# Every engine takes the computed order: one manually scheduled region around a whole attention and MLP kernel

## The chip, the core and the metric

The kernel runs on one core of a Trainium2 chip. Five engines work side by side, each through its own list of instructions: TensorE (PE, matrix products, with its weight loads PEld), VectorE (DVE), ScalarE (ACT), GpSimd (POOL) and SyncE (SP, here only the issue of DMAs). They wait for each other through semaphores. Each engine takes the instructions of its list in the order in which they stand there, so an instruction that waits holds up all that stand behind it on its engine.

The metric is the device time of one execution in microseconds (us), as the median of several runs; lower is better.

## What is computed

Linear attention with random features over 8 batches, 8 heads, 576 positions and head size 64, and an MLP with a Silu over the result, all in float32:

```python
def phi(x):
    proj = np.einsum('bhsd,md->bhsm', x, omega)          # 128 features
    h = proj - np.sum(x * x, axis=-1, keepdims=True) / 2.0
    h = h - np.max(h, axis=-1, keepdims=True)
    return np.exp(h) / np.sqrt(m)
q_p, k_p = (phi(q_s), phi(k_s))                          # q, k scaled by D ** -0.25
kv = np.einsum('bhsm,bhsd->bhmd', k_p, v)
z = np.sum(k_p, axis=2)
num = np.einsum('bhsm,bhmd->bhsd', q_p, kv)
den = np.einsum('bhsm,bhm->bhs', q_p, z)[..., None] + 1e-06
attn = num / den
...
x = attn.transpose(0, 2, 1, 3).reshape(B * S, H * D)     # 4608 x 512
h = x @ w_in                                             # 512 x 2048
g = h * (1.0 / (1.0 + np.exp(-h)))
out = g @ w_out                                          # 2048 x 512
```

## The kernel before

The attention is cut into 32 windows, one for a batch and a pair of heads. A window goes through these steps, each a small function: load `raw` (k and q, transposed, line 238), `nat` (k and q by rows, 242) and `v` (246) on SP; squares on ACT (250) and their row sums on DVE (254); the projection on PE (262, and 269 for the middle block); row maxima (276, 278) and the shift `nb` (282, 283) on DVE; the exponentials on ACT (298, from window 8 on 312); the sums of k's features over the positions on POOL (318 to 323) and their product with ones on PE, `z` (327), copied by ACT into `zb` (335, 336); `kv` on PE (343), copied into `kt` (348), turned (351) and copied into `kw` (356); the products of q's features with z on DVE (362), their sums `den` and reciprocals `rd` (369, 370); the normalization on POOL (375); three transposes on PE (381), copied into `en` (385); and the numerator (399), which ACT and DVE split into a high and a low part `xh`, `xl` (413, 418).

Four windows give the input of one block of 512 rows of the MLP, so there are eight blocks, and a ninth from the rests of 64 rows (`rest`, 423, stored and loaded again). A block takes 16 steps, one for each 128 columns of `w_in`: stage 1 (495, twelve matmuls into `ps_h`), Silu twice on ACT (500 for the high part `gh`, 501 in place), the low part `gl` on DVE (505), and two steps later stage 2 (513, twelve matmuls into `ps_acc`). In the first block the weights are prepared too: load `wraw` on SP (435), exponent on ACT (442), three DVE instructions (456, 458, 462), split on POOL into `wh`, `wl` (or `wp`, which is stored, 483, and fetched for every step, 487).

ACT needs a table load to go from an exponential to a Silu or back.

What sets the order: about 3,600 units (`add(name, engine, duration, due, ...)`) go to a planner, the class `Plan`. It walks through time with a free time for each engine, looks at what each unit needs and which buffers are free, and gives back one list of all units. The kernel then emits the units in that list's order. Before the change this is not yet the order on the engines: the library's scheduler takes the emitted instructions, with the emission as a priority, and decides by its own model of when things are ready what stands where on each engine.

Of the kernel before, what the change touches and what calls it, by code (L numbers as in the profile page):

```python
# [197 lines left out]
def attention_mlp(ctx: ExitStack, tc: tile.TileContext, qT, kT, qn, kn, v, om_in, w_in, w_out, out):  # L198
# [6 lines left out]
    pools = {  # L205
        p: ctx.enter_context(tc.tile_pool(name=f"ps_{p}", bufs=RINGS[p], space=PSUM)) for p in ("acc", "h", "att")
    }
# [13 lines left out]
    def bank(pool):  # L221
        return pools[pool].tile([P, 512], F32, tag=pool, name=f"ps_{pool}")
# [310 lines left out]
    plan = Plan()  # L533
# [155 lines left out]
    for i, (t, f) in enumerate(steps):  # L689
# [16 lines left out]
        for j in range(4):  # L706
# [11 lines left out]
            if f == NF - 1:  # L718
                add(("store", t, j), "ACT", 0.62, k2 + 0.2, lambda t=t, j=j: store(t, j), after=[("s2", t, f, j)],
                    free=[("po", t, j)])  # L720
    for u in plan.run():
        u["fn"](*[bank(p) for p in u["pools"]])


_OUT = ((B * S, DMODEL), "float32")
# [48 lines left out]
```

## Time and profile before

| | us |
|---|---|
| median of 3 runs | 1099.16 (1097.70 to 1101.51) |
| profiled execution | 1101.4 |
| its span, from the first to the last instruction | 1099.3 |
| PE busy | 1053.1 (96%) |
| DVE busy | 566.4 (52%) |
| ACT busy | 583.1 (53%) |
| POOL busy | 255.5 (23%) |

An engine's busy time is the union of its instructions' times. In a row of instructions in order of time the first number is the start in us from the span's start, the second the length of the row; then engine, line, operation, the tile written and the tiles read, and in brackets the idle time of the engine just before it and whose event ended it. A row of waits gives the sum of the waits, their count and the longest one. ACT's table loads number 48 at line 312, 56 at line 500, 11 at line 298, 4 at line 501 and 1 at line 232.

### The profile page before, as it was taken

Reading aid. Unit: us, or ns where it says so; the run is one execution under the profiler, and the core shown is the slowest. Engines: PE = TensorE matmul, PEld = TensorE weight load, DVE = VectorE, ACT = ScalarE, POOL = GpSimd, SP = SyncE. Lnnn points to the kernel's source line nnn. Section 1 sums busy time; section 2 is a strip of 40 time slices with the busy share of each in tenths; the row PEclk is TensorE's granted clock in tenths of the full one; section 3 lists DMA queues with packets and bytes.
Section 4 is the critical chain, followed back from the end, with each engine's and each line's share of the span. In section 5 each row is a group of like instructions: output and inputs, shape, how many; then the busy total and the mean of one; then the engine's idle time right before and its main releaser. Section 6 shows DMA issues by size and latency. Waiting matters only on the chain.

```text
span 1099.3 us, 16192 instructions
## 1 busy us (share of the span) xinstructions
PE 1053.1 (96%) x5900; PEld 834.5 (76%) x5900; DVE 566.4 (52%) x1109; ACT 583.1 (53%) x1085; POOL 255.5 (23%) x327
## 2 busy tenths in 40 slices
PE   5677998899999999999999999999999999999998
PEld 4455776687877778777778777787877788888886
DVE  6788897745555455545555455555554431111111
ACT  5557878565556555555556555655565442222211
POOL 3666665411111111111111111111111110000000
PEclk7688999999999999999999999999999999999999
DMA  7576787553335443444345433533343226223323
GB/s 282 198 221 234 265 290 252 182 167 125 124 126 178 139 133 119 136 165 138 122 139 178 140 127 130 173 131 126 123 154 104 80 80 213 96 96 122 109 96 96
DMA packets 66526, 167.84 MB, mean 153 GB/s; under 512 B 15632, under 2 KB 15760, under 8 KB 66448
## 3 DMA queue, kind: packets, MB, share of 16 engines
q1 hardware_dynamic: 65984, 166.23, 45.6%
q8 instruction: 47, 0.77, 0.3%
q10 hardware_dynamic: 464, 0.59, 0.1%
q14 instruction: 31, 0.25, 0.1%
HBM read 146.87 MB, written 19.92 MB: 152 GB/s over the span
## 4 chain that ended last, share of the span: by engine, by line
PE 86%; DVE 5%; DMA 3%; ACT 3%; POOL 1%; issue 1%; SPq 0%; ACTq 0%; DVEq 0%; POOLq 0%
PE ps_acc L513 35%; PE ps_h L495 34%; PE ps_att L262 5%; PE ps_att L343 3%; PE ps_att L381 3%; PE ps_att L399 2%; DMA wraw<-w_out 1%; DMA nat<-qn 1%; PE ps_att L327 1%; PE ps_att L269 1%; DVE w L458 1%; ACT hq L298 1%; DVE w L462 1%; POOL hq L375 1%; DVE den L369 1%
## 5 line engine op out<-in xcount | busy, mean ns | idle before, releaser
L513 PE MATMUL ps_acc<-wo,gh 128*128 128x512 f32 x1152 | 369.9, 402 | 0.0
L500 ACT ACTIVATE gh<-ps_h 128x512 fp32r<-128x512 f32 x144 | 86.2, 599 | 295.9 <-PE ps_h L495 295.3
L505 DVE TENSOR_TENSOR gl<-ps_h,gh 128x512 fp32r<-128x512 f32 x144 | 99.1, 688 | 275.8 <-ACT ps_h L501 275.8
L513 PEld LDWEIGHTS ps_acc<-wo,gh 128*128 128x128 f32 x1152 | 207.1, 189 | 43.7
L495 PE MATMUL ps_h<-xh,wh 128*128 128x512 f32 x576 | 235.0, 409 | 0.3 <-ACT xh L413 0.3
L495 PE MATMUL ps_h<-xh,wl 128*128 128x512 f32 x576 | 226.7, 394 | 0.0
L495 PE MATMUL ps_h<-xl,wh 128*128 128x512 f32 x576 | 225.9, 392 | 0.0
L513 PE MATMUL ps_acc<-wo,gl 128*128 128x512 f32 x576 | 225.8, 392 | 0.0
L375 POOL TENSOR_TENSOR hq<-hq,rd 128x384 f32<-128x384 f32 x96 | 81.7, 879 | 421.4 <-DVE rd L370 396.5
L495 PEld LDWEIGHTS ps_h<-xh,wh 128*128 128x128 f32 x576 | 108.1, 188 | 24.7 <-issue 0.8
L513 PEld LDWEIGHTS ps_acc<-wo,gl 128*128 128x128 f32 x576 | 108.1, 188 | 24.2 <-issue 0.8
L495 PEld LDWEIGHTS ps_h<-xh,wl 128*128 128x128 f32 x576 | 108.1, 188 | 24.1
L495 PEld LDWEIGHTS ps_h<-xl,wh 128*128 128x128 f32 x576 | 108.5, 188 | 22.3 <-DVE xl L418 0.4
L312 ACT ACT_TABLE_LOAD x48 | 61.6, 1283 | 69.2 <-DVE hq L303 53.3
L318 POOL TENSOR_TENSOR t<-hk 128x256 f32<-128x256 f32 x64 | 48.8, 780 | 183.2 <-ACT hk L312 170.1
L278 DVE TENSOR_REDUCE mxq<-ps_att 128x4 f32<-128x512 f32 x57 | 37.2, 687 | 99.7 <-PE ps_att L262 99.6
L501 ACT ACTIVATE ps_h<-ps_h 128x512 f32<-128x512 f32 x144 | 85.3, 593 | 0.0
L500 ACT ACT_TABLE_LOAD x56 | 71.8, 1283 | 22.0 <-PE ps_h L495 21.3
L362 DVE TENSOR_TENSOR prod<-hq,zb 128x512 f32<-128x512 f32 (+1 forms) x96 | 52.3, 595 | 49.6 <-ACT zb L336 47.7
L250 ACT ACTIVATE nat<-nat 128x576 f32<-128x576 f32 x64 | 44.6, 703 | 20.3 <-DMA nat<-kn 12.3
L381 PE MATMUL ps_att<-ident,hq 128*128 128x128 f32 x261 | 41.1, 284 | 7.9 <-POOL wp L476 2.4
L278 DVE TENSOR_REDUCE mxk<-ps_att 128x4 f32<-128x512 f32 x55 | 35.6, 686 | 18.7 <-PE ps_att L262 18.7
(121 smaller groups left out, 1232.0 us busy)
## 6 DMA issues: line engine op xcount, KB each, us to landing
wo<-wo_d SPq DMA_DIRECT2D x144, 512.0 KB, 3.3
rawk<-kT SPq DMA_DIRECT2D x32, 352.0 KB, 3.0
rawq<-qT SPq DMA_DIRECT2D x32, 352.0 KB, 3.8
v<-v SPq DMA_DIRECT2D x32, 320.0 KB, 2.9
nat<-kn SPq DMA_DIRECT2D x32, 288.0 KB, 3.3
nat<-qn SPq DMA_DIRECT2D x32, 288.0 KB, 3.2
wraw<-w_in SPq DMA_DIRECT2D x16, 512.0 KB, 4.6
wraw<-w_out SPq DMA_DIRECT2D x16, 512.0 KB, 4.3
```

Source lines behind the costliest of these rows:

```text
L262: nc.tensor.matmul(ps[:, i * M : (i + 1) * M], raw[r, o : o + P], oms[r], start=True, stop=True)
L278: nc.vector.tensor_reduce(m[:, 5 * j : 5 * j + 4], ps.rearrange("p (c m) -> p c m", m=M), AX.X, ALU.max)
L312: nc.scalar.activation(h, h, AF.Exp)
L318: nc.gpsimd.tensor_tensor(t[:, j], e[:, 5 * j : 5 * j + 2], e[:, 5 * j + 2 : 5 * j + 4], ALU.add)
L362: nc.vector.tensor_tensor(prod[:, c, :M], e[:, c], zb[:, j].unsqueeze(1).broadcast_to([P, hi - lo, M]), ALU.mult)
L375: nc.gpsimd.tensor_tensor(e[:, c], e[:, c], rd[:, c].unsqueeze(2).broadcast_to([P, 3, M]), ALU.mult)
L381: nc.tensor.transpose(ps[:, i * P : (i + 1) * P], T["h", n, "q"][:, 3 * g + i], ident)
L495: nc.tensor.matmul(ph, w[:, k, :], x, start=k == 0 and n == 0, stop=k == NK - 1 and n == 2)
L500: nc.scalar.activation(gh, ph, AF.Silu)
L501: nc.scalar.activation(ph, ph, AF.Silu)
L505: nc.vector.tensor_tensor(gl, T["ph", t, f], T["gh", t, f].bitcast(F32), ALU.subtract)
L513: nc.tensor.matmul(T["po", t][j], g[:, js], w, start=f == 0 and n == 0, stop=f == NF - 1 and n == 2)
```

## The change

The loop that emits the units goes into one region of the library in which every engine issues its instructions in the order of emission. Nothing else differs; the planner, its costs and its list are the same.

```diff
-    for u in plan.run():
-        u["fn"](*[bank(p) for p in u["pools"]])
+    with tc.manual_schedule():
+        for u in plan.run():
+            u["fn"](*[bank(p) for p in u["pools"]])
```

So the planner's list now stands on every engine, where the library's scheduler had moved units or parts of units. From the middle of the second MLP block on the two orders are almost the same on PE, ACT and POOL; most differences lie in the first block and ahead of it. Three places:

PE, the list's rows near its start, where the transposes of window 0 (line 381) end and window 1 goes on; `es` are POOL's sums, `kt` the copy of kv. Before:

```order
L381 MATMUL ps_h<-ident,hq 128x128 x3
L381 MATMUL ps_att<-ident,hq 128x128 x6
L327 MATMUL ps_h<-es,ones 128x256
L343 MATMUL ps_att<-hk,v 64x128 x10
L399 MATMUL ps_acc<-en,kw 64x512 x2
L399 MATMUL ps_att<-en,kw 64x64 x2
L262 MATMUL ps_acc<-oms,rawk 128x128 x8
L351 MATMUL ps_acc<-ident,kt 128x128
```

and now:

```order
L381 MATMUL ps_h<-ident,hq 128x128 x3
L381 MATMUL ps_att<-ident,hq 128x128 x6
L343 MATMUL ps_att<-hk,v 64x128 x10
L399 MATMUL ps_acc<-en,kw 64x512 x2
L399 MATMUL ps_att<-en,kw 64x64 x2
L262 MATMUL ps_acc<-oms,rawk 128x128 x8
L351 MATMUL ps_acc<-ident,kt 128x128
L327 MATMUL ps_h<-es,ones 128x256
```

The z product of window 1 (line 327) stood ahead of kv, of the numerator of window 0 and of the projection of window 2's k; now it stands behind them and behind the turn of kv.

ACT, windows 3 and 4; the squares (line 250) are those of q of window 6, `kt` and `kw` are window 4's. Before:

```order
L298 ACTIVATE hk<-ps_acc,nbk 128x128
L250 ACTIVATE nat<-nat 128x576
L348 COPY kt<-ps_acc 128x128
L356 COPY kw<-ps_acc 128x128
L298 ACTIVATE hq<-ps_att,nbq 128x128 x8
L385 COPY en<-ps_att 128x384
```

and now:

```order
L298 ACTIVATE hk<-ps_acc,nbk 128x128
L348 COPY kt<-ps_acc 128x128
L298 ACTIVATE hq<-ps_att,nbq 128x128 x8
L385 COPY en<-ps_att 128x384
L356 COPY kw<-ps_acc 128x128
L385 COPY en<-ps_att 128x384 x2
```

The square is gone from here (it stands behind the numerator's copies, lines 413, now), and `kw` goes behind the eight exponentials.

ACT, window 6 and steps 6 and 7 of the first MLP block; `hk` is the exponential of the middle block. Before:

```order
L500 ACT_TABLE_LOAD
L500 ACTIVATE gh<-ps_h 128x512
L298 ACT_TABLE_LOAD
L298 ACTIVATE hk<-ps_att,nbk 128x128
L501 ACT_TABLE_LOAD
L501 ACTIVATE ps_h<-ps_h 128x512
L385 COPY en<-ps_att 128x384
```

and now:

```order
L298 ACTIVATE hk<-ps_att,nbk 128x128
L500 ACT_TABLE_LOAD
L500 ACTIVATE gh<-ps_h 128x512
L501 ACTIVATE ps_h<-ps_h 128x512
L385 COPY en<-ps_att 128x384
```

The exponential stood between the two Silu activations of a step; now the pair stays together. This happened in four steps; no such place is left, and ACT has eight table loads fewer.

In words, on the other engines: on DVE `den` of window 2 (line 369) stood behind the square sum of window 4's q (line 254), and now stands ahead of it; the two DVE rows of `nb`, and `den` and `rd`, stood apart with other rows between them, and now stand together. On POOL the five rows of a window's sums had weight rows between them in windows 1, 4, 5 and 6, and now have none. On PE six matmuls of line 495 of step 1 stood ahead of the transposes of window 2, and now stand behind two of the three of window 4. On SP some loads of `raw`, `v` and `nat` and the stores of `rest` change places with the loads of weights.

## The prediction, made before the changed kernel ran

> **What bounds the kernel now.** I read the page's busy shares first, then the busy time by stage, then who waits for whom on TensorE, and last the instructions in order of time around each long wait.
>
> ```profile
> PE 1053.1 (96%) x5900; PEld 834.5 (76%) x5900; DVE 566.4 (52%) x1109; ACT 583.1 (53%) x1085; POOL 255.5 (23%) x327
> ```
>
> TensorE (PE) is the bound over the whole. Whether it is so everywhere, the stages tell (from and to, the length, then PE's busy time and matmuls, weight loads, DVE, ACT, POOL, the granted clock of TensorE and the share of the DMA engines):
>
> ```profile
> 28.20:101.10 72.90, 51.36 (x316) 34.54 (x317) 59.75 (x108) 44.50 (x134) 48.42 (x55) 0.76 0.66 213
> ...
> 118.30:216.00 97.70, 89.43 (x495) 67.28 (x494) 82.84 (x137) 72.34 (x137) 59.54 (x60) 1.00 0.72 247
> 245.60:1086.00 840.40, 840.19 (x4693) 675.38 (x4693) 374.88 (x767) 412.15 (x704) 122.73 (x179) 1.00 0.40 130
> ```
>
> From 245.6 to 1086 us PE lacks 0.2 us of 840.4. Nothing that leaves its work alone can make that shorter, and its rows stand in nearly the same order in both kernels. What can be had lies ahead of it: 72.90 - 51.36 = 21.5 us of PE idle time in the first row and 97.70 - 89.43 = 8.3 in the second. The time up to 28.2 us has the same order on every engine but for pairs that change nothing for PE. So the question is how many of these 29.8 us the new order takes away, and whether it adds others. The two longest single waits of PE after 28 us (in all, times, longest) are ended by POOL's sums and by one of ACT's copies:
>
> ```profile
> PE ps_h L327 <- POOL es L323: 5.5, 1, 5.5
> PE ps_acc L351 <- ACT kt L348: 3.0, 1, 3.0
> ```
>
> **The change, place by place.** No instruction is added but markers, and PE, DVE and POOL do the same work. Every term is therefore a wait of one engine's row for another, and each is a question of what stands ahead of what.
>
> *Term 1, window 1.* PE has the z product of window 1 (line 327) ahead of the kv and numerator products, and it waits for POOL's sums:
>
> ```profile
> 33.65 1.22 PE L327 MATMUL ps_h<-es,ones 128*128 128x256 f32 x2 [5.50 <-POOL es L323]
> ...
> 45.43 0.90 PE L381 MATMUL ps_acc<-ident,hq 128*128 128x128 f32 x3 [2.69 <-POOL hq L375]
> ```
>
> In the new order kv, the numerator and the next projection come first and fill those 5.50 us. The sums end when they did (POOL's rows up to them only change places), so z still starts at 33.65; what it feeds comes earlier, because ScalarE's (ACT) copies of z stood behind `kt`, which waited for kv:
>
> ```profile
> 37.25 0.27 ACT L348 COPY kt<-ps_att 128x128 f32<-128x128 f32 x1 [6.71 <-PE ps_att L343]
> ...
> 39.92 0.27 ACT L336 COPY zb<-ps_h 128x128 f32<-128x128 f32 x1
> ...
> 42.33 1.35 DVE L369 TENSOR_REDUCE den<-prod 128x9 f32<-128x1161 f32 x1
> ...
> 44.20 0.21 DVE L370 RECIPROCAL rd<-den 128x9 f32<-128x9 f32 x1
> ```
>
> z ends at 33.65 + 1.22 = 34.87; four copies take about 1.1 (0.27 each), so 35.9. The three products take 1.59 when they stand together (the row of window 2 below), to 37.5, then `den` 1.35, so `rd` can start near 38.8 where it stood at 44.20: 5.4 us earlier, and with it POOL's three normalizations and the transposes at 45.43. PE's own wait gives the same size from the other side (5.50). **5.4 us.**
>
> *Term 2, window 2.* VectorE (DVE) has the square sum of a later window ahead of `den`, and that one waits, by way of ACT's square, for a load that the chain of what ended last shows (its start, its length):
>
> ```profile
> 53.83 4.20 DMA nat<-qn
> ...
> 55.83 1.59 DVE L362 TENSOR_TENSOR prod<-hq,zb 128x512 f32<-128x512 f32 x3
> 58.83 0.76 DVE L254 TENSOR_REDUCE sqq<-nat 128x9 f32<-128x576 f32 x1 [1.41 <-ACT nat L250]
> 59.50 1.35 DVE L369 TENSOR_REDUCE den<-prod 128x9 f32<-128x1161 f32 x1
> ...
> 61.37 0.20 DVE L370 RECIPROCAL rd<-den 128x9 f32<-128x9 f32 x1
> ```
>
> In the new order `den` and `rd` follow the products at once: `rd` at 57.42 + 1.27 (1.35 less the overlap of 0.08 that these rows show) = 58.7 instead of 61.37, **2.7 us**. The load's lateness then falls on the square sum, which is wanted only by the exponentials two windows on. Against it stands that PE filled a part of this wait with six matmuls of line 495, which the new order puts later:
>
> ```profile
> 57.68:59.23 1.55, 1.55 (x7) 0.94 (x5) 0.40 (x1) 1.01 (x2) 0.00 (x0) 1.00 0.83 164
> ```
>
> They fill the 1.55 us of this stretch (the seventh runs in from before) and are still to be done: **minus 1.5**.
>
> *Term 3, window 4.* ACT has a square (line 250), whose load lands late, ahead of the copy `kt` (line 348), for which PE's line 351 waits:
>
> ```profile
> 84.22 0.68 ACT L250 ACTIVATE nat<-nat 128x576 f32<-128x576 f32 x1 [4.07 <-DVE mxk L278]
> 84.81 0.25 ACT L348 COPY kt<-ps_acc 128x128 f32<-128x128 f32 x1
> ...
> 80.76 1.31 PE L343 MATMUL ps_acc<-hk,v 128*64 128x128 f32 x20
> ```
>
> The kv products end at 82.07, so `kt` can run there and not at 84.81: **2.7 us**, and the square goes behind, where its load has long landed. What is late next is the exponential of the same window's q, about 2 us behind; the three transposes after it keep a wait.
>
> Up to 101 us that is 5.4 + 2.7 - 1.5 + 2.7 = 9.3 of the 21.5 us of idle time. From 101.1 to 118.3 PE was full and stays so.
>
> *Term 4, windows 5 to 7 (118 to 216 us).* ACT's pair of Silu activations (lines 500, 501) is torn apart four times by one exponential, and a pair torn apart costs two table loads more:
>
> ```profile
> L501 ACT ACT_TABLE_LOAD  x4: 1283/1283/1283, 139.5 to 190.4; - x4
> ```
>
> In the new order no pair is torn apart: 8 x 1.283 = 10.3 us of ACT's time go. How much of it PE sees, no row tells; the bounds are 0 (ACT is busy 72 of 97.7 us, and the idle time may come from elsewhere) and the 8.3 us that PE idles there. Neither end is nearer to a row, so I take the middle, **4.1**.
>
> Costs that I put at nothing: dependent pairs on DVE now stand back to back; DVE is busy 375 of 840 us where PE is full, which hides them. SP's loads move by one to four places; what that can cost is rival 4.
>
> Sum: 9.3 + 4.1 = 13.4 us. The profiled execution took 1101.4 us (span 1099.3 and 2.1 around it), so it would be 1088.0; the median of the runs is 1099.16, 2.2 below it, which gives 1085.8. **I forecast 1086.**
>
> **A rule weighed.** DVE's first product of window 6 took far longer than its second, which has the same form, while POOL worked beside it:
>
> ```profile
> 150.18 1.75 DVE L362 TENSOR_TENSOR prod<-hq,zb 128x512 f32<-128x512 f32 x1 [0.64 <-ACT zb L336]
> ...
> 152.05 0.68 DVE L362 TENSOR_TENSOR prod<-hq,zb 128x512 f32<-128x512 f32 x1
> ```
>
> The Trainium skill, page "SBUF — State Buffer", section "Who interferes with whom", says that the port pair which DVE and GpSimd share is an exclusive lock: a DVE instruction with two SBUF inputs and a GpSimd instruction do not share it, the later one waits to the end. The trace agrees in kind (1.75 against 0.68). By that rule the change has a price of its own, since the same DVE and POOL work is packed into fewer microseconds; it would bring about the first rival.
>
> **The rivals.**
>
> *1. The weights set the pace.* Between 118 and 216 us DVE is busy 82.84 of 97.7 us, mostly with the words of the weights, and POOL makes of them what PE reads. If DVE and POOL finish no weight earlier than now, step 13 of the MLP cannot start before its weight:
>
> ```profile
> 181.58 1.30 POOL L480 TENSOR_TENSOR wl<-w,wh 128x512 fp32r<-128x512 f32 x1
> ...
> 191.40 0.50 PE L495 MATMUL ps_h<-xh,wh 128*128 128x512 f32 x1
> ```
>
> 191.40 - 182.88 = 8.5 us is then all that can be gained: 1099.2 - 8.5 = 1090.7, and 1095 where a product row's excess of 1.07 us (1.75 - 0.68, above) is paid once more in each of four windows. Against it: DVE also gets free time back, since rows that waited for loads no longer block it.
>
> *2. More than I count.* If the new order removes all 8.3 us after 118 and 5 of the 12.2 us that I leave before 101, the gain is 9.3 + 8.3 + 5 = 22.6: 1076.6.
>
> *3. The wait only moves.* PE meets the window's normalizations later instead of the sums, with the chain over DVE and POOL as long as before: 1099. Against it: `rd` is shown above to be late because of its neighbours, not of its own inputs.
>
> *4. Slower: SP's queue.* In the new order SP's loads of raw q and the stores of `rest` stand ahead of weight loads that now pass them (the stores of `rest` of window 5 ahead of three, the load of `rawq` of window 8 ahead of one). These wait in the same stretch (101 to 216 us) for:
>
> ```profile
> SPq L238 <- PE ps_att L269: 13.9, 5, 5.2
> ...
> SPq L423 <- DVE xl L418: 4.0, 3, 2.1
> ```
>
> If all 17.9 us came on top of the weights' times, step 13 would start at 182.9 + 17.9 = 200.8 instead of 191.4: 9.4 us later, 1108.6. It decides from 8.5 + 3.3 = 11.8 us of added delay on. Against it: SP waits for mid products that themselves come earlier.
>
> That the change does nothing can be left out: the order differs on all five engines.
>
> **How the numbers follow.** Chances: the forecast with its own range 1081 to 1091, 0.60; rival 1, 0.18; rival 2, 0.10; rival 3, 0.05; rival 4, 0.07. A measurement of this kernel can tell about 0.3% from no change, 3.3 us, so faster is below 1095.9 and slower above 1102.5. The forecast and rivals 1 and 2 are faster: 0.88; same 0.05; slower 0.07. The range takes in rivals 1 and 2 and leaves 3 and 4 out: 1076.5 to 1096.5.
>
> **What would show it.** Term 1: no idle time before line 327, and the transposes of window 1 near 40 instead of 45.4 us. Term 2: `rd` right behind `den` in window 2, some 8 us earlier than 61.4 with term 1. Term 3: `kt` of window 4 right behind kv. Term 4: no table load at line 501, and PE idle time of about 4 us where it was 8.3. From there to the end PE must be full and as long as before, 840 us from the numerator of window 8 on; if that stretch is longer, the new order has a wait in every window and I am wrong in the part that I held safe. Rival 4 would show as idle time before line 495 or 513 with a DMA or POOL's weights as its end.

## The result, and the profile after

The changed kernel takes **1090.57 us** (median of 4 runs, 1089.20 to 1091.57) where the kernel before, on the same chip, took 1099.2: a ratio of 0.992, with a 95% interval of 0.9907 to 0.9933. That is 8.6 us where 13.4 had been worked out. The profiled execution took 1089.6 us, its span is 1087.5. Busy times of the whole, from the page:

```profile
PE 1040.2 (96%) x5900; PEld 825.2 (76%) x5900; DVE 572.1 (53%) x1109; ACT 574.3 (53%) x1077; POOL 254.6 (23%) x327
```

ACT has eight instructions fewer, the table loads. PE has the same 5900 matmuls and is busy 12.9 us less (1053.1 before). The stages of the changed kernel, in the columns of the prediction (from and to, length, busy time of PE, PEld, DVE, ACT, POOL, granted clock, DMA share, GB/s):

```profile
28.20:94.50 66.30, 44.78 (x301) 31.04 (x298) 64.95 (x106) 46.41 (x137) 43.83 (x50) 0.74 0.70 227
...
111.50:203.90 92.40, 84.15 (x495) 64.07 (x494) 83.67 (x138) 62.49 (x130) 56.87 (x59) 1.00 0.75 252
233.10:1073.50 840.40, 839.68 (x4694) 673.37 (x4694) 367.76 (x767) 414.31 (x704) 122.75 (x179) 1.00 0.41 130
```

Three things are to be seen. The last row is as long as before: the part held safe was safe. The first row is 6.6 us shorter, and DVE is now busy 64.95 of its 66.30 us (98%; 59.75 of 72.90 before). And in the second row PE's idle time is what it was: 92.40 - 84.15 = 8.25 us, before 97.70 - 89.43 = 8.27. The row is 5.3 us shorter because the *same 495 matmuls take 5.3 us less busy time*. The prediction had asked only for idle time. The first row has the idle time that it had, too: 66.30 - 44.78 = 21.52 us, before 72.90 - 51.36 = 21.54. But its two stretches hold 301 and 316 matmuls; a comparison over the same matmuls stands in the part on why the prediction was right.

Which matmuls? The same stretches again, with the busy time of the projections (line 262) alone, before and then after:

```profile
118.30:216.00 97.70, 11.29 (x96) 1.00 0.72 247
```

```profile
111.50:203.90 92.40, 7.24 (x96) 1.00 0.75 252
```

4.05 of the 5.3 us are there. A projection is eight calls, emitted in pairs: for each of four groups of columns one for the first head and one for the second, which read rows 0 to 63 and rows 64 to 127 (`r = slice(j * D, (j + 1) * D)`). The trace has two matmuls for a call, so 16 for a projection; this stretch holds three projections of k and three of q. PE's rows of a projection of q before,

```profile
139.70 1.16 PE L262 MATMUL ps_att<-oms,rawq 64*128 64x128 f32 x8
140.78 0.50 PE L495 MATMUL ps_h<-xh,wl 128*128 128x512 f32 x1
...
142.05 0.40 PE L495 MATMUL ps_h<-xl,wh 128*128 128x512 f32 x1
142.38 1.16 PE L262 MATMUL ps_att<-oms,rawq 64*128 64x128 f32 x8
```

and now:

```profile
192.63 0.39 PE L495 MATMUL ps_h<-xh,wl 128*128 128x512 f32 x1
192.95 1.16 PE L262 MATMUL ps_att<-oms,rawq 64*128 64x128 f32 x16
194.04 0.50 PE L495 MATMUL ps_h<-xh,wh 128*128 128x512 f32 x1
```

In the three projections of q the library's scheduler had pulled the two heads apart, with matmuls of line 495 between them: eight of one head take 1.16 us, twice. In the order of emission the heads alternate, and sixteen take the same 1.16 us (1.43 in the slowest projection of this stretch): a matmul in one half of the array's rows runs beside one in the other half. The Trainium skill says so, in "TensorE: Matmul & The Clock Gate", section "Part 3: Packing small matmuls — row/col tiling": matmuls whose operands sit in different rows of the array overlap. These rows agree: twice the matmuls in the same 1.16 us. Nothing in the forecast had used it.

The places that the prediction named, in the changed kernel (a timeline):

```profile
32.17 0.70 PE L327 MATMUL ps_h<-es,ones 128*128 128x256 f32 x2 [0.70 <-POOL es L323]
...
38.58 0.90 PE L381 MATMUL ps_acc<-ident,hq 128*128 128x128 f32 x3 [3.27 <-POOL hq L375]
...
52.86 1.36 DVE L369 TENSOR_REDUCE den<-prod 128x9 f32<-128x1161 f32 x1
54.26 0.21 DVE L370 RECIPROCAL rd<-den 128x9 f32<-128x9 f32 x1
...
74.34 0.27 ACT L348 COPY kt<-ps_acc 128x128 f32<-128x128 f32 x1 [2.71 <-PE ps_acc L343]
```

All of these came: z's wait is 0.70 us instead of 5.50, the transposes of window 1 start 6.9 us earlier, `rd` of window 2 stands behind `den` and 7.1 us earlier, `kt` of window 4 follows kv at once. What did not come is the fourth sign, PE idle time of about 4 us in the second row: it is 8.25. Behind the wait for POOL's `hq`, the longest in sum before (the first row below), PE's longest waits from 28 to 245 us (sum, count, longest) are now ended by DVE. The row of before, then the four of the changed kernel:

```profile
PE ps_acc L381 <- POOL hq L375: 8.0, 5, 3.4
```

```profile
PE ps_acc L381 <- POOL hq L375: 6.9, 4, 3.3
PE ps_h L495 <- DVE xl L418: 2.9, 1, 2.9
PE ps_att L327 <- DVE hq L306: 2.4, 1, 2.4
PE ps_att L269 <- DVE xl L418: 2.4, 1, 2.4
```

### The profile page after: what moved, and what is told of

Its sections match the earlier page's. It is cut to its first block, busy times and chain, and to the rows that moved or that the text cites. A ratio compares the mean times of both kernels' runs of the same rounds, so it can differ in the third digit from the quotient of the medians.

```text
span 1087.5 us, 16156 instructions
## 1 busy us (share of the span) xinstructions
PE 1040.2 (96%) x5900; PEld 825.2 (76%) x5900; DVE 572.1 (53%) x1109; ACT 574.3 (53%) x1077; POOL 254.6 (23%) x327
## 4 chain that ended last, share of the span: by engine, by line
PE 80%; DVE 9%; ACT 6%; DMA 2%; issue 2%; POOL 0%; ACTq 0%; SPq 0%; DVEq 0%; POOLq 0%
PE ps_h L495 33%; PE ps_acc L513 32%; PE ps_att L262 5%; PE ps_att L343 3%; PE ps_att L381 2%; PE ps_att L399 2%; DVE w L458 1%; PE ps_att L327 1%; ACT L500 1%; DVE w L462 1%; PE ps_att L269 1%; DVE w L456 1%; DMA out<-ot 1%; DVE prod L362 1%; DMA wo_d<-wp 1%
## 5 line engine op out<-in xcount | busy, mean ns | idle before, releaser
L495 PE MATMUL ps_h<-xh,wh 128*128 128x512 f32 x576 | 237.7, 413 | 0.3 <-ACT xh L413 0.3
L375 POOL TENSOR_TENSOR hq<-hq,rd 128x384 f32<-128x384 f32 x96 | 78.5, 846 | 380.0 <-DVE rd L370 375.3
L495 PEld LDWEIGHTS ps_h<-xh,wh 128*128 128x128 f32 x576 | 108.6, 189 | 24.8 <-ACT xh L413 0.5
L495 PEld LDWEIGHTS ps_h<-xh,wl 128*128 128x128 f32 x576 | 108.6, 188 | 24.5
L250 ACT ACTIVATE nat<-nat 128x576 f32<-128x576 f32 x64 | 44.3, 700 | 23.4 <-DMA nat<-kn 18.6
```

Source lines behind the costliest of these rows:

```text
L375: nc.gpsimd.tensor_tensor(e[:, c], e[:, c], rd[:, c].unsqueeze(2).broadcast_to([P, 3, M]), ALU.mult)
L495: nc.tensor.matmul(ph, w[:, k, :], x, start=k == 0 and n == 0, stop=k == NK - 1 and n == 2)
```

## The experiments

The regions below are cut out of the planner's list by the planner's own time (`at`). The table puts all profiles side by side, with two of the kernel before and of two others. Its columns: where the numerator of window 4 begins (its first matmul of line 399, in us), the time from the numerator of window 3 to that of window 4, the time from there to the numerator of window 8, PE's idle time and line 262's part of PE's busy time in that last stretch, and the time of the whole. They are worked out from the traces' single records; each stretch has the same matmuls in every kernel but for four moved across its start in *dveonly*. Some expectations count window 4 from the kv products just ahead of the numerator, about 1 us earlier. The granted clock in the stretch from window 4 to window 8 was 0.97 in *before, again*, *nodve* and *dveonly* and 0.98 to 1.00 in the others, so a part of the three's matmul time there can be the clock's.

| kernel | w4 | w3 to w4 | w4 to w8 | idle | L262 | time |
|---|---|---|---|---|---|---|
| before | 119.4 | 29.4 | 127.3 | 8.4 | 13.2 | 1099.2 |
| before, again | 116.7 | 29.5 | 127.9 | 6.1 | 14.5 | |
| changed | 112.6 | 31.7 | 121.7 | 8.4 | 9.0 | 1090.6 |
| changed, again | 113.1 | 32.3 | 123.0 | 8.3 | 9.0 | |
| early | 116.0 | 36.2 | 123.0 | 4.6 | 13.5 | 1094.7 |
| late | 117.3 | 29.5 | 121.8 | 7.2 | 9.0 | 1094.6 |
| nodve | 110.3 | 28.8 | 128.3 | 10.9 | 11.0 | 1094.8 |
| nodve, again | 110.7 | 28.8 | 128.9 | 13.1 | 9.9 | |
| dveonly | 116.7 | 33.7 | 129.1 | 10.3 | 12.9 | 1100.6 |
| hybrid95 | 114.2 | 30.3 | 120.4 | 7.4 | 9.0 | 1089.6 |
| hybrid_tail | 111.8 | 29.9 | 120.1 | 7.4 | 8.9 | 1088.2 |
| nosign | 106.6 | 29.8 | 117.6 | 4.0 | 8.7 | 1078.5 |
| nosign_b | 108.6 | 27.7 | 124.9 | 5.0 | 13.7 | 1089.9 |
| nopool | 108.4 | 29.8 | 114.0 | 2.6 | 8.7 | 1077.7 |

**Half the change at a time.** The region for the units planned before 95 us alone, and for those from 95 us on alone.

```diff
+    order = plan.run()
+    cut = next(i for i, u in enumerate(order) if u["at"] >= 95.0)
     with tc.manual_schedule():
-        for u in plan.run():
+        for u in order[:cut]:
             u["fn"](*[bank(p) for p in u["pools"]])
+    for u in order[cut:]:
+        u["fn"](*[bank(p) for p in u["pools"]])
```

(*late* has the region around the second loop instead.)

> The manual region holds only the units that the plan starts before 95 us (attention of windows 0 to 4 and the first MLP step); the rest goes to the library's scheduler as before. In the profiles of before and after, the numerator of window 4 starts 6.8 us earlier with the change, and the rest of the lead (12.5 at window 8) comes behind it. Theory L (each stretch's gain is its own): about 1099.2 - 0.55 x 8.6 = 1094.5, with the numerator of window 4 near 111.5 and the table loads at line 501 back, 4 of them. Rival (the later stretch sets the pace whatever comes ahead): within 2 of 1099.

> The other half: the region holds only the units that the plan starts from 95 us on. Theory L: about 1099.2 - 0.45 x 8.6 = 1095.3, the numerator of window 4 near 118.3 as before, no table load at line 501, and 4 to 5 us of lead won between windows 4 and 8. Rival (the early lead is what makes the later one possible): within 2 of 1099.

Measured: 1094.71 us, ratio 0.9965 (0.9952 to 0.9979), and 1094.59, ratio 0.9961 (0.9946 to 0.9975). The gains are 4.2 and 4.3 us, in sum 8.5, the whole. But the table warns against reading them as two places. *late* wins in windows 4 to 8, where its projections are paired (9.0 us). *early* leaves those torn (13.5) and wins there too, by less idle time, while its window 4 comes hardly earlier than in the second profile of before: what an order wins early can show late. The expectation of *early* (window 4 near 111.5) missed; the two times came as theory L had them.

**Which engine's order.** The region can be told which engines it holds; the others stay with the scheduler.

```diff
-    with tc.manual_schedule():
+    with tc.manual_schedule(engines={ET.PE, ET.Activation, ET.Pool, ET.SP}):
```

(*dveonly* holds `ET.DVE` alone.)

> The region orders PE, ACT, POOL and SP; DVE's order is the scheduler's. Theory D (in the changed kernel DVE bounds the stretch from 28 to 94 us, busy 65 of 66 us, and dependent pairs that stand back to back cost it 3 us there at line 283 alone): the pairs are apart again, so 2 to 4 us less than the changed kernel, 1087 to 1089, and line 283 at its former mean of 0.3 us up to 95 us instead of 0.56. Rival T (DVE's order itself brought the gain, the sums of window 2 ahead of a square sum that waits): 1092 to 1095.

> The region orders DVE alone; the four other engines' orders are the scheduler's. Theory D: at best the 2.7 us of the prediction's term 2 less what the back-to-back pairs cost: 1097 to 1100. Rival T (DVE's order is what brought the gain): 1091 to 1094.

Measured: *nodve* 1094.82 us, ratio 0.9959 (0.9944 to 0.9975); *dveonly* 1100.57, ratio 1.0018 (1.0009 to 1.0028), a loss. DVE's planned order alone brings nothing. But it is worth some 4 us (1094.8 to 1090.6) when the others are in order: without it windows 4 to 8 take 6.6 us longer, of which 2.5 are PE's idle time and 2.0 the projections. So theory D's 1087 to 1089 for *nodve* missed, and the time is rival T's. In the stretch from window 3 to window 4 it is the other way round, 28.8 us with DVE free and 31.7 with DVE bound (*dveonly* 33.7). The two stretches from the windows view, *nodve* and then the changed kernel:

```profile
81.40:110.30 28.90, 26.41 (x137) 19.25 (x138) 26.16 (x45) 25.60 (x52) 19.55 (x20) 0.91 0.78 267
```

```profile
80.80:112.60 31.80, 27.03 (x135) 19.76 (x136) 31.07 (x45) 25.62 (x52) 20.87 (x21) 0.86 0.72 241
```

For the same number of instructions (45) DVE is busy 31.07 us, all but 0.7 of the stretch, instead of 26.16. The products with z grew, here in *nodve* and then in the changed kernel, whose sixth starts behind the stretch (count, busy time, mean ns):

```profile
L362 DVE TENSOR_TENSOR prod<-hq,zb 128x512 f32<-128x512 f32 (+1 forms) x6 | 3.4, 626 | 1.1 <-ACT zb L336 1.1
```

```profile
L362 DVE TENSOR_TENSOR prod<-hq,zb 128x512 f32<-128x512 f32 (+1 forms) x5 | 5.2, 1087 | 0.3 <-ACT zb L336 0.3
```

The second profile of each kernel has 627 and 1090 ns. The tiny instructions of `nb` (lines 282, 283) grew too: by the single records they take 0.25 us in the mean in both profiles of *nodve*, and 0.74 and 0.66 in those of the changed kernel.

**DVE free early, bound late.**

```diff
+    with tc.manual_schedule(engines={ET.PE, ET.Activation, ET.Pool, ET.SP}):
+        for u in order[:cut]:
...
+    with tc.manual_schedule():
+        for u in order[cut:]:
```

> Two regions: up to the units that the plan starts before 95 us it orders PE, ACT, POOL and SP and leaves DVE to the scheduler, from there on all five. With DVE left to the scheduler throughout, the numerator of window 4 started at 109.1 us (111.5 with the change, 118.3 before), and 4.4 us were lost again between windows 6 and 7. Theory D (the plan's order on DVE is dear ahead of 95 us and good behind it): both gains together, the numerator of window 4 near 109, of window 8 near 231, time 1088 to 1089. Rival (the lead of 2.4 us is swallowed by the weights in the stretch behind, which DVE fills to 90%): 1090 to 1091, as the changed kernel.

Measured: 1089.58 us, ratio 0.9908 (0.9893 to 0.9922). It keeps *late*'s stretch (120.4) and most of *nodve*'s (30.3), yet the total is only 1 us below the changed kernel's, less than the runs can tell, and lies between the theory's 1088 to 1089 and the rival's 1090 to 1091. Its window 4 comes 4 us later than expected; *hybrid_tail*, whose order is the same up to there, has it 2.5 us earlier.

**Less work on DVE.** The sign is left out of the weights (32 instructions of line 462), so the MLP computes with their absolute values; in the changed kernel and in the one before.

```diff
         else:
-            nc.vector.scalar_tensor_tensor(bits, high, 0x80000000, bits, ALU.bitwise_and, ALU.bitwise_or)
```

> The changed kernel without the third DVE instruction on each block of weights (line 462, which sets the sign; 32 instructions of 0.7 to 1.2 us on DVE; ten of them ahead of 95 us, 8.7 us in the changed kernel's profile). Theory D (DVE bounds the stretch up to 95 us in the changed kernel): a large part of these 8.7 us goes, the numerator of window 4 starts 4 to 8 us earlier than 111.5, and the time falls to 1081 to 1086. Rival C (the chain over PE, ACT and POOL bounds it, DVE is only busy beside it): 0 to 2 us, 1088 to 1091.

> The same instruction left out of the kernel before. There DVE is busy 60 of 73 us up to 101 us and PE's waits are ended by loads and by other engines. Theory D: half or less of what it brings in the changed kernel up to window 4: the numerator of window 4 0 to 4 us ahead of 118.3, time 1094 to 1099. Rival C: the same gain in both kernels.

Measured: 1078.48 and 1089.91 us, 12.1 and 9.6 us less than with the sign (ratio of the first to before 0.981). So the work on the weights' words, which has nothing to do with the order, sets the pace up to window 8 in both kernels. Up to window 4 the kernel before gains more by it (8.1 to 10.9 us, by which profile is taken) than the changed one (6.0 to 6.6), so the expectation that it would matter half as much or less before was wrong, and rival C (the same gain in both) is nearer; with two runs each, 12.1 and 9.6 are not told apart. The instruction left out is also a step of the chain from a weight's load to PE: whether DVE's free time or the earlier weight brings the gain isn't separated.

**How far one profile can be trusted.** The kernel before, the changed one and *nodve*, unaltered, once more.

> The kernel before, profiled once more. The profiled executions of before and after lie 11.8 us apart, the medians 8.6. If the first profile of before was a slow one in its own stretch up to 245 us, this one starts the numerator of window 8 some 2 us ahead of 245.6; if the spread lies behind, at 245.6 with another length of the rest.

> The changed kernel, unaltered, once more: a second profile of it, since two profiles of the kernel before differ by 2.8 us in where the numerator of window 4 begins (119.44 and 116.65 us) and by 2.2 at that of window 8. If the early stretch falls short of the 9.3 us of the prediction for a reason that lies in the order (VectorE is full there), the numerator of window 4 begins at 111.5 to 113.5 us again, as in the first profile (112.60), and VectorE is busy over 97% from 28.2 to 94.5 us. If the shortfall was the scatter of one profile, it begins at 110.5 or earlier and VectorE has 2 us or more of idle time there.

> The region without VectorE, unaltered, once more. Its first profile had the numerator of window 4 at 110.26 us and that of window 8 at 238.56. If VectorE's free choice of its next instruction really is worth 2 us up to window 4 and costs 4 us from window 6 on, both come again: 110 to 111 and 238 to 239. If the first was scatter, the numerator of window 4 comes at 112 or later.

Measured: window 4 moves by 2.8 us between the profiles of before, by 0.5 and 0.4 between those of the others. The changed kernel's shortfall and DVE's 96.8% from 28.2 to 94.5 us came again, just short of the 97% that was written down; so did both sides of *nodve* (110.7 and 239.6, the second just outside of its 238 to 239). The one run of each took 1099.26, 1091.53 and 1093.93 us. The forecast was read off the later of the two profiles of before. A part of the scatter arises ahead of the change's places: up to 28.2 us the granted clock was 0.76 in the first profile of before and 0.84 in the second, and the numerator of window 0 begins at 37.0 and 35.2 us. *hybrid95* and *hybrid_tail* have 0.76 and 0.83 there, and 30.5 and 28.4 us. That the clock is the cause isn't shown (the changed kernel's two profiles, 0.76 and 0.85, have 29.0 and 28.4), but the column w4 carries this scatter, while the column from window 3 to window 4 repeats within 0.6 us.

**GpSimd beside DVE.** Its two instructions on a weight become memsets that read nothing, so the MLP's weights are constants.

```diff
-        nc.gpsimd.tensor_copy(parts_of(i)[0], T["w", i])
+        nc.gpsimd.memset(parts_of(i)[0].bitcast(F32), 0.01)
...
-        nc.gpsimd.tensor_tensor(lo, T["w", i], hi.bitcast(F32), ALU.subtract)
+        nc.gpsimd.memset(lo.bitcast(F32), 0.001)
```

> The changed kernel with GpSimd's two instructions on a weight (lines 476 and 480) replaced by memsets of the same tiles, which read nothing; so the weights of the MLP are constants and its output is not the reference's. Theory: VectorE's two-input instructions are held up by GpSimd's beside them. Then VectorE's products with z (line 362) take 0.65 us or less in the mean from 28 to 94.5 us, where they took 0.78, line 458 0.8 or less where it took 1.05, VectorE's busy time there falls by 5 us or more, and the numerator of window 4 begins by 108 us. Rival: VectorE is simply full of work of the same length; then these means stay within 0.05 us, VectorE's busy time falls by less than 2 us, and the numerator of window 4 moves by less than 2 us from 112.6. In the late stretch the weights come earlier under both. Should memsets hold VectorE up as the old instructions did, the means stay too: the lengths of VectorE's instructions inside and outside of GpSimd's memsets tell that.

Measured: 1077.68 us in one run. Four of the costlier groups on DVE (count, busy time, mean ns), from 28.2 to 101.1 us before, then from 28.2 to 94.5 in the changed kernel, then in *nopool*:

```profile
L462 DVE SCALAR_TENSOR_TENSOR w<-wraw,w 128x512 uint32<-128x512 uint32 x10 | 10.4, 1065 | 0.0
...
L362 DVE TENSOR_TENSOR prod<-hq,zb 128x512 f32<-128x512 f32 (+1 forms) x12 | 6.5, 583 | 0.6 <-ACT zb L336 0.6
L458 DVE SCALAR_TENSOR_TENSOR w<-wre,w 128x512 uint32<-128x512 uint32 x8 | 6.3, 796 | 0.0
...
L283 DVE SCALAR_TENSOR_TENSOR nbk<-nbk,sqk 128x9 f32<-128x9 f32 (+2 forms) x6 | 1.9, 324 | 0.0
```

```profile
L362 DVE TENSOR_TENSOR prod<-hq,zb 128x512 f32<-128x512 f32 (+1 forms) x12 | 8.7, 780 | 0.1
L458 DVE SCALAR_TENSOR_TENSOR w<-wre,w 128x512 uint32<-128x512 uint32 x8 | 8.4, 1054 | 0.1
...
L462 DVE SCALAR_TENSOR_TENSOR w<-wraw,w 128x512 uint32<-128x512 uint32 x8 | 6.8, 849 | 0.3
...
L283 DVE SCALAR_TENSOR_TENSOR nbk<-nbk,sqk 128x9 f32<-128x9 f32 (+2 forms) x6 | 3.8, 632 | 0.2
```

```profile
L458 DVE SCALAR_TENSOR_TENSOR w<-wre,w 128x512 uint32<-128x512 uint32 x10 | 9.0, 897 | 0.1
L462 DVE SCALAR_TENSOR_TENSOR w<-wraw,w 128x512 uint32<-128x512 uint32 x10 | 7.9, 790 | 0.3
...
L362 DVE TENSOR_TENSOR prod<-hq,zb 128x512 f32<-128x512 f32 (+1 forms) x12 | 6.2, 568 | 0.0
...
L283 DVE SCALAR_TENSOR_TENSOR nbk<-nbk,sqk 128x9 f32<-128x9 f32 (+2 forms) x6 | 3.2, 535 | 0.2
```

Packed more tightly, some of the same instructions are longer: the mean product by 34%, the step of line 458 by 32%, the tiny `nb` of k twice as long. Others are shorter: the step of line 462 by 20%, so that the three steps on a block of weights (with line 456, 793 and then 763 ns) take 2.65 us before and 2.67 now. And the second profiles have mean products of 673 and 816 ns, 21% apart. With GpSimd's reads gone the product falls to 0.57 us as expected; line 458 falls only to 0.90 (0.8 was expected), DVE's busy time by 3.0 us (5 expected), window 4 comes at 108.4 (108 expected). In the stretch from window 3 to window 4, where *nodve* was shown above, the products take 0.55 us here, near to *nodve*'s 0.63 and far from the changed kernel's 1.09: another order on DVE, or no reads of weights on GpSimd, either takes their length away. That fits a length that arises where the order puts them beside those reads. The `nb` of q fall too (0.16 us here), but the two of k stay at 0.81 and 0.75 us as in the changed kernel, and only *nodve*'s order shortens them (0.10 and 0.39). The rival (same lengths) is out, but the sizes fall short. How much of the 13 us comes from DVE's lengths and how much from GpSimd's own, shorter instructions isn't separated.

**The parts that won, and the tail.** *hybrid95*, with the last stores outside of the region.

```diff
+    end = next(i for i, u in enumerate(order) if u["name"][0] == "store" and u["name"][1] == B)
...
+        for u in order[cut:end]:
...
+    for u in order[end:]:
+        u["fn"](*[bank(p) for p in u["pools"]])
```

> A version put together from the parts that won: TensorE, ScalarE, GpSimd and SyncE in the planner's order and VectorE free up to the planner's 95 us, then all five in its order, and the last stores of the ninth block outside of the region. In the changed kernel ScalarE issues a store of one output tile ahead of its copy for the next, and that copy and VectorE's alternate in single steps: 5.5 us from TensorE's last matmul to the end, where the kernel before has 4.5. If this order is what costs 1.0 us, the end comes 4.5 us after TensorE's last matmul (in the other hybrid 5.5), and the time is 1088.5, a ratio to before of 0.990. If the tail is set by the stores' own way to memory, it stays at 5.5 and the time at 1089.5. The difference of the totals is too small to be told apart by the rounds; the profile's tail decides.

Measured: 1088.19 us (1086.38 to 1091.24), ratio 0.9912 (0.9895 to 0.9930): the best median, but not told apart from the changed kernel. From PE's last matmul to the end it takes 5.0 us, halfway: 4.5 before, 5.5 in the changed kernel and *hybrid95*. In the end of *hybrid95* ScalarE's store stands ahead of its own copy:

```profile
1082.70 0.50 ACTq L531 DMA_DIRECT2D out<-ot  x1
1083.30 0.37 ACT L527 COPY ot<-ps_acc 128x256 f32<-128x256 f32 x1 [1.08 <-DVE ot L528]
```

In that of *hybrid_tail* the copy stands ahead of both stores:

```profile
1079.69 0.37 ACT L527 COPY ot<-ps_acc 128x256 f32<-128x256 f32 x1 [0.45 <-PE ps_acc L513]
1079.77 1.36 ACTq L531 DMA_DIRECT2D out<-ot  x2
```

From PE's last matmul to the end of DVE's last copy it takes 0.9 us before and in *hybrid_tail*, and 1.6 in the changed kernel and *hybrid95*: this order costs 0.6 us. What follows, with the last stores' way to memory, takes 3.6, 4.1, 3.9 and 4.0 us in these four, and 3.5 in *nopool*, which has the changed kernel's order; so it varies with the order unchanged.

## Why the prediction was right, and where it was not

The direction and the place were right: all of the gain lies ahead of window 8, and the stretch from there to PE's end took 848.0 us before and 847.7 after. That the time fell into the forecast's own range of 1081 to 1091, at its upper end, owes something to luck, as the terms show. By two profiles each, the gain is 5.2 us up to the numerator of window 4 (118.0 to 112.9 in the mean; 3.5 to 6.8 by which pair is taken), 5.3 from there to window 8, 0.3 behind it, less 1.0 in the tail: 9.8 us between the profiles, 8.6 between the medians.

**Terms 1 to 3, 9.3 us, mis-sized: 5.2 measured, and less than half of that as idle time.** The stretch from the start to the numerator of window 4 holds the same matmuls in both kernels; the two profiles of before, then the two of the changed kernel, in the columns of the prediction:

```profile
0.00:119.44 119.44, 86.21 (x527) 62.41 (x529) 92.17 (x170) 78.42 (x213) 67.80 (x80) 0.79 0.71 236
```

```profile
0.00:116.65 116.65, 82.92 (x526) 60.29 (x528) 93.82 (x170) 77.79 (x213) 69.31 (x80) 0.82 0.73 242
```

```profile
0.00:112.60 112.60, 79.84 (x526) 58.91 (x528) 102.09 (x167) 78.13 (x213) 68.10 (x80) 0.79 0.74 247
```

```profile
0.00:113.13 113.13, 82.19 (x527) 61.30 (x529) 102.72 (x167) 78.71 (x213) 67.22 (x80) 0.80 0.73 248
```

PE's idle time was 33.2 and 33.7 us and is 32.8 and 30.9, in the mean 1.6 us less (0.5 to 2.8 by which pair is taken), where terms 1 to 3 are waits and would take away 9.3; the other 3.6 of the 5.2 us are busy time, which differs by up to 3.3 us between two profiles of one kernel. Lines 262 and 399 alone are busy 2.6 and 2.4 us less, in the mean; other lines take back a part, and no run separates them. DVE is busy 9.4 us more for three instructions fewer. Each local reading of the prediction held (z started 1.5 us earlier than it said), and at window 3's numerator the gain was 6.3 to 9.3 us. It was given back between windows 3 and 4, which take 31.7 and 32.3 us instead of 29.4, because DVE had become the bound. The step that failed is "Costs that I put at nothing: dependent pairs on DVE now stand back to back; DVE is busy 375 of 840 us where PE is full, which hides them". The cover was named for the wrong stage: in this one DVE had 59.75 of 72.90 us, and some of its instructions then grew longer. Freeing DVE's order alone (*nodve*) takes the loss away (28.8 us in both profiles), and at window 4 it gains 7.6 us by two profiles each (9.2 against the first profile of before, the one that the forecast was read off); so the order of DVE is shown to be the cause of the loss there. That GpSimd's reads lengthen some of DVE's instructions is shown by *nopool*, where the same stretch takes 29.8 us; what share of these 3 us is theirs is not shown, since its weights also come earlier.

**Term 4, 4.1 us: the size came, the mechanism did not.** The eight table loads went (line 501 has none, line 298 has 7 instead of 11), but PE's idle time in the stretch stayed at 8.25 where 8.27 was: other waits, for DVE's `hq` and `xl`, took their place. What went is matmul time, 4.05 us of it in the projections. That the size agrees with the 4.1, the middle between two bounds, is luck. The step that failed is "PE, DVE and POOL do the same work. Every term is therefore a wait": the same matmuls cost less beside the right neighbour. The same is to be seen over the whole kernel: PE's idle time was 46.2 us and, in the second profile, 44.3, and is 47.3 and 45.4 now, a rise as large as the tail's 1.0, while its busy time fell from 1053.1 and 1052.8 us to 1040.2 and 1044.0. It was there to be seen in the order, which kept the pairs apart before. In the table line 262 takes 8.7 to 9.0 us in all seven profiles with every engine in planned order from 95 us on, 9.9 and 11.0 with DVE free, and 12.9 to 14.5 where the scheduler orders PE. No run paired the projections and changed nothing else, so their share of the total is read from the traces, not isolated.

**The rule that was weighed** (the Trainium skill, "SBUF — State Buffer", "Who interferes with whom": an instruction with two SBUF inputs on DVE and one on GpSimd that reads SBUF wait for each other) fits a part of it: with GpSimd's reads replaced, the mean product falls from 0.780 to 0.568 us.

**The rivals.** Rival 1 named 1090.7 us, which is the time that came, and its theme was right: the work on the weights sets the pace (*nosign*, *nopool*). Its place was wrong, so the number agrees by luck. The weight of step 13 was ready at 179.1 us instead of 182.9 and waited 3.0 us for PE, so PE did not stand there for its weight, and no wait of line 495 for one stands among PE's waits from 28 to 245 us. That the pace comes through DVE's queue, in which `xl`, `hq` and `nb` stand behind the weights' words, is read from PE's waits for DVE and not shown by a run. Rival 2's further 8 us weren't there, rival 3 was wrong at once, and rival 4 did not come: no DMA ends one of PE's longer waits. The tail's 1.0 us stood in no term.

## What to carry to other kernels

Taking away PE's waits one by one gives a gain only until the next engine is full: look at every engine's busy share in *that* stage, not in the whole. And compare busy times of the same instructions before and after, not only idle times: here the order set how long the matmuls on half of the array's rows took (8 or 16 in 1.16 us), and how long DVE's products beside GpSimd took (0.63 or 1.09 us in one stretch). An order can be fixed for some engines and some stages only, and the second profile of an unchanged kernel tells how much of a difference between two profiles is there at all.

## What was unexpected of the hardware

Two streams of eight matmuls on 64 rows each take 1.16 us together when they alternate, and 1.16 us each when they don't. An instruction of DVE on at most 128x9 elements took 0.32 us in the mean in one order and 0.63 in another. And an unaltered kernel reached the same place 2.8 us earlier in a second profile, while its time differed by 2.
